# Scores from 40 rows a head and products on halves of 64 output rows, with a new list of first steps, in an mLSTM and feed-forward kernel

## The chip, the cores and the metric

The kernel runs on one core of a Trainium2 chip. The metric is device time of one execution in microseconds (us). The kernel before takes 456.23 us as the median of three runs (455.87 to 456.26). Lower is better.

## The reference

Two layers. The first is an mLSTM with 4 batches, 8 heads, 768 steps and a head size of 40; the second a feed-forward layer over its 3072 rows of 320 features, with 2048 hidden ones. Cut to what is computed:

```python
for t in range(S):                                   # S = 768
    m_new = np.maximum(f_gate[:, :, t] + m, i_gate[:, :, t])
    f_stab = np.exp(f_gate[:, :, t] + m - m_new)
    i_stab = np.exp(i_gate[:, :, t] - m_new)
    C = f_stab * C + i_stab * einsum('bhd,bhe->bhde', vt, kt)    # state, 40 x 40 a head
    n = f_stab * n + i_stab * kt
    h_tilde = einsum('bhde,bhe->bhd', C, qt)
    denom = np.maximum(np.abs(einsum('bhd,bhd->bh', n, qt)), 1.0)
    y[:, :, t] = sigmoid(o_gate[:, :, t]) * h_tilde / denom
x = y.transpose(0, 2, 1, 3).reshape(3072, 320)
h = x @ w_in                                         # 320 x 2048
out = (np.maximum(h, 0) + alpha * np.minimum(h, 0)) @ w_out      # 2048 x 320
```

All results are float32; the weights w_in and w_out come as float64.

## The kernel before

The steps over time are cut into chunks of 128 tokens: 6 chunks a batch, 24 in all. Inside a chunk the recurrence becomes products of matrices: scores (K times Q, 128 x 128 for each of 8 heads), weighed by a matrix of decays E, times the values; and a state part, Q times the state C that the chunks before left. Two chunks make a group of 256 tokens, for which the feed-forward layer is computed: products with the upper weights (`ph`, 8 pairs of hidden blocks, fp32r in parts), relu, and products with the lower weights (`po`).

The first six chunks (the first batch) are computed in f32 directly; the later ones from bf16 parts. The change touches the first six only. For them:

- Q and K of a chunk are transposed by pairs of heads on TensorE (steps qT and kT, tile `pqk`) and copied out by ScalarE (qc, kc). A pair's two heads stand in rows 0 to 39 and 64 to 103. Q goes to the tile `qf` whole. K goes to a padded tile `kf` with a place for each head of the pair: `padded_copy` writes the first head's 64 rows and the second head's 40 rows with two copies, and `padded_tiles` (step kfz) filled the other rows with zeros once.
- `scores(n, par)` (steps sc) multiplies K of one head of each pair, padded to 104 rows, with Q: four matmuls for each of the two heads of the pairs, in two separate steps. VectorE weighs them with E (wg).
- `values` (steps v) multiplies E, 128 rows by 128 columns, with the values `va` of 42 columns, for eight heads into one tile `pH`.
- `from_state` (steps fm, ft) multiplies `qf` with the state C of a pair, 84 columns, into `pI`.
- `products` (steps um, uc; tile `pu`) updates the state. It writes the two heads of a pair to rows 0 to 39 and 64 to 103 of its output. The change doesn't touch it.

The order of all instructions of each engine is written out by hand: `ORDER` lists steps by name, `PATTERN` goes on for the later groups, and `pin` ties each engine to that order. So an instruction that waits holds back everything behind it on its engine. Names in the list: dq, dv, dL, do are loads of q and k, of values, of the decay rows `Lb` and of the output gate; iXY, rX and oX with d, s, x, y, j, h, l or others behind them load a block of w_in or w_out (d), and take it apart from float64 (passes on ScalarE and VectorE, tiles `t_wi`, `t_wr`, `t_wo`) into high and low parts (h, l). U, R, S, G, K are the five steps of a feed-forward block of a group, D its lower products; warm2 are two matmuls on constants into a tile that nothing reads. i01 is the load into tile `wi_1` of the first rows, o4 and o3 are two blocks of w_out.

All loads stand on one queue, SP's, in the order of the list.

Of the kernel before, what the change touches and what calls it, by code (L numbers as in the profile page):

```python
# [8 lines left out]
F32 = mybir.dt.float32  # L9
# [8 lines left out]
def kernel(ctx: ExitStack, tc: tile.TileContext, q, k, v, i_gate, f_gate, o_gate, w_in, w_out, alpha, out):  # L18
    nc = tc.nc
    B, H, S, D = q.shape  # L20
    DM, DFF = w_in.shape
    P = 128
# [316 lines left out]
    def values(n, E, busy=lambda: None):  # L339

        pH = psa(f"pH{n}")
        dense(pH, FILL.get(n, 0))
        va = va_t[n // GC % NV][:, n % GC]
        for i in range(H):
            if i % 2 == 0:
                busy()
            par, p = divmod(i, NPR)
            h = 2 * p + par
            nc.tensor.matmul(  # L349
                pH[:, h * VA : (h + 1) * VA], E[par][:, p * P : (p + 1) * P], va[:, h], start=True, stop=True  # L350
            )
        return pH[:, : H * VA].rearrange("p (h e) -> p h e", e=VA)
# [48 lines left out]
    def from_state(n, qf, Q=None):  # L401
# [237 lines left out]
    def row_of(g, fp, e):  # L639
# [12 lines left out]
    FILL = {}  # L652
    ORDER = """warm14 dq0 Cz warm2 warm2 warm2 qT0 warm2 sca0 lf0a kT0 i00d lf0z lf0b li0 L0 sca1 bj0 dq1 warm2 qc0 lqa lqb kc0 lqc lqd sp01 eeL i00s
        lf1a lqe wt0 warm2 warm2 warm2 qT1 qc1 bTt bTc ex01 warm2 sp00 warm2 warm2 sp11 r0d lf1b ewj wTt wTc ex00 warm2
        sp10 ex11 kT1 i00y L1 li1 do0 dv0 kfz i01d eTt ex10 wd0 dq2 gma i00j sc00 o0d lpa sc01 um0 kc1 gmd gmm sc11
        eTc eel bj1 og1 r0s uc0 fm1 wtl wg01 sc10 ewl lpb i11d wd1 alT wg00 gmc qT2 i01s glt ft1 wg10 glc alC dL lpc
        lpd lpe qc2 warm2 wg11 dv1 um1 uc1 i00h i01x i01j kT2 kc2 i00p o0s o0x sp20 v0 r0y r0j gr0 sp21 fm2 dq3 ex20
        warm2 o0j r0h i01h ft2 i01p ex21 o0h warm2 gg0 r0l gx0 i11s sc20 wg20 v1 ta1 gr1 qT3 qc3 i11x gp0 x0 xa0 sc21
        dL4 gg1 gx1 gp1 kT3 wg21 x1 xa1 o1d wd3 xd0 r0H xd1 wd2 sq30 ey30 r0L i11j ex40 o0l F0 U00 i20d i10d R00 S00
        kc3 v2 ta2 um2 uc2 o1s o1y U01 dq4 i10s i10x i10j sq31 gr2 o1j i11k i11l ey31 qT4 G00 ex41 fm3 ft3 sc30 K00  # L660
        wg30 i10h um3 uc3 D00 R01 kT4 i20s do1 S01 qc4 wd4 kc4 o1h i20x sc31 wg31 dv2 um4 uc4 i20j og2 o2d i20h gg2
        i10p fm4 o1l o5d sc41 wg41 G01 K01 i21d gx2 r2d sc40 i20p o2s o2x dq5 wg40 o5s o5x v3 ta3 o2j gr3 gg3 o2h o5j
        r2s dL5 o4d r2x o2l U02 o3d r2j gx3 gp3 R02 gp2 i21s v4 ft4 ta4 qT5 qc5 r2H ex50 r2h r2p U03 x2 R03 S02 G02 x3
        dq6 i21y i21j r2L i31d fm5 ft5 xa2 xd2 i21h i21p dv3 i30d kT5 kc5 K02 S03 o4s o4y D01 G03 wd6 K03 o3s o3y o3j
        D02 do2 dL7 ex51 o7d o4j o6d U04 R04 S04 o3h xa3 V05 r05 o3p o4h sc50 o4p sc51 G04 i31s i31x xd3 s05 wg51 um6
        uc6 K04 gr4 wg50 F1 U10 U11 R10 S10 og3 gg4 gx4 dL6 gp4 R11 S11 G10 o5h o5p v5 K10 D10 U12 ta5 G11 g05 K11 vp0
        i31j i30s i30x gr5 gg5 U13 i31h i30j R12 i30h D11 S12 i31l G12 gx5 gp5 K12 D12 R13 dq7 S13 o7s i30l U06 o7x
        do3 o7j N05 G13 K13 D13 tp0 o6s tp1 o6x R06 tp2 x4 x5 o6j o6h vp1 U07 o7h tp3 D03 D04 D05 R07 S06 G06 S07 o6l
        xa5 xd5 xa4 xd4 G07 K06 K07 D06 o7l D07 Z0"""
    PATTERN = """og.-1 V4<< tf.1 vb.1 xn.-1 xp.-1 V5<< tg.1 g2<< N2<< vc.1 r4<< vb.0 th.1 ti.1 s4<< g3<< r5<< s0.0 s1.0 ua.0 ub.0  # L670
# [270 lines left out]
    def first_group():  # L941
# [140 lines left out]

        def scores(n, par):
            if n >= GC:
                ps = psa(f"pS{n}_{par}")
            elif n * par == 0:
                ps = ps_h.tile([P, 512], F32, tag="h", name=f"pS{n}_{par}")
            else:
                ps = ps_o.tile([P, 512], F32, tag="o1", name=f"pS{n}_{par}")
# [97 lines left out]
        def decay_parts(k, tag):  # L1187
# [35 lines left out]
        def values_of(n):  # L1223
            got["h", n] = values(n, [E[n, 0], E[n, 1]])
# [5 lines left out]
        def chunk_steps(n):  # L1230

            steps[f"wd{n}"] = lambda: weighed(n)
            steps[f"v{n}"] = lambda: values_of(n)
            steps[f"ta{n}"] = lambda: added(n)
# [8 lines left out]
            for par in range(2):  # L1243
# [121 lines left out]
```

## Time and profile before

| | |
|---|---|
| median of three runs | 456.23 us (455.87 to 456.26) |
| the profiled execution | 456.2 us |
| its span, first to last instruction | 454.5 us |
| TensorE busy | 448.2 us, 99% of the span |
| TensorE weight loads busy | 438.8 us, 97% |
| VectorE, ScalarE, GpSimd busy | 310.9, 314.9, 312.6 us (68%, 69%, 69%) |
| granted clock of TensorE, mean | 0.998 |
| moved by DMA | 61.60 MB, mean 136 GB/s |

Busy shares of the whole span are means over two very different stages. In the first some 85 us the first batch is computed while all weights are loaded and taken apart; then the pattern of the later groups repeats. A matmul of the trace lasts until its modelled end, which lies behind the next one's start, so a block's cost is read from its start to the start of the next block. An f32 matmul stands as two records in the trace, an fp32r or bf16 one as one.

### The profile page before, as it was taken

To read this page: it belongs to the slowest core of one execution; us is meant where nothing else is said; L and a number is where in the kernel's file an instruction comes from. 1 tells how busy PE (TensorE), PEld (TensorE's weight loads), DVE (VectorE), ACT (ScalarE), POOL (GpSimd) and SP (SyncE) were. 2 spreads that over 40 slices of the span, in tenths; PEclk is the share of its full clock that TensorE was granted. 3 is DMA by queue.
4 is the path that set the end of the run, shared out by engine and by line. 5 is a ranking of instruction groups with operands and counts; after the bars stand their busy time and mean duration, and the time that the engine had idled before them with its cause. 6 is when DMAs were issued, how large, how long until landed. Compare 5 with 4: busy or idle time off the path is not lost.

```text
span 454.5 us, 11766 instructions
## 1 busy us (share of the span) xinstructions
PE 448.2 (99%) x4418; PEld 438.8 (97%) x4418; DVE 310.9 (68%) x659; ACT 314.9 (69%) x717; POOL 312.6 (69%) x400
## 2 busy tenths in 40 slices
PE   8999999999999999999999999999999999999996
PEld 6789999999999999999999999999999999999996
DVE  4798999558866767767767767767767767753321
ACT  5999997959767767758768758658758668433331
POOL 7836566737889698588798698597798696143231
PEclk9999999999999999999999999999999999999999
DMA  8999998769674575597783783589682451000000
GB/s 182 248 253 214 232 232 226 139 143 180 156 168 110 137 160 104 133 184 163 121 183 103 131 179 105 115 188 180 128 168 86 97 142 40 1 30 1 30 1 29
DMA packets 156162, 61.60 MB, mean 136 GB/s; under 512 B 140154, under 2 KB 145834, under 8 KB 156106
## 3 DMA queue, kind: packets, MB, share of 16 engines
q1 hardware_dynamic: 156026, 60.75, 59.9%
q8 instruction: 35, 0.57, 0.5%
q14 instruction: 21, 0.17, 0.1%
q10 hardware_dynamic: 80, 0.11, 0.1%
HBM read 36.90 MB, written 4.03 MB: 90 GB/s over the span
## 4 chain that ended last, share of the span: by engine, by line
PE 91%; ACT 4%; DVE 3%; POOL 1%; issue 1%; POOLq 0%; DVEq 0%; ACTq 0%
PE po L771 36%; PE ph L734 5%; PE ph L739 5%; PE ph L735 5%; PE ph L736 5%; PE ph L741 5%; PE ph L737 5%; PE ph L740 5%; PE ph L738 5%; PE pH L390 4%; PE pS L491 4%; PE pu L192 2%; PE px L600 2%; PE pS L1092 2%; PE pH L349 2%; PE pI L415 1%
## 5 line engine op out<-in xcount | busy, mean ns | idle before, releaser
L760 POOL TENSOR_TENSOR gl<-g,gh 128x512 fp32r<-128x512 f32 x74 | 96.1, 1301 | 32.5 <-ACT gh L758 31.3
L744 ACT ACTIVATE g<-ph 128x512 f32<-128x512 f32 x96 | 57.3, 597 | 81.7 <-PE ph L741 79.7
L771 PE MATMUL po<-OH,gh 128*128 128x320 f32 x368 | 111.3, 314 | 0.0
L771 PE MATMUL po<-OL,gh 128*128 128x320 f32 x368 | 108.7, 308 | 0.0
L749 DVE SCALAR_TENSOR_TENSOR g<-g,oma,ph 128x256 f32<-128x256 f32 x148 | 63.6, 471 | 65.5 <-ACT g L744 64.1
L771 PEld LDWEIGHTS po<-OH,gh 128*128 128x128 f32 x368 | 69.2, 188 | 0.0
L771 PEld LDWEIGHTS po<-OL,gh 128*128 128x128 f32 x368 | 69.2, 188 | 0.0
L771 PE MATMUL po<-OH,gl 128*128 128x320 f32 x368 | 68.8, 308 | 0.0
L771 PEld LDWEIGHTS po<-OH,gl 128*128 128x128 f32 x368 | 57.5, 188 | 0.3 <-DVE gl L760 0.3
L734 PE MATMUL ph<-XH,WH 128*128 128x256 f32 x192 | 54.1, 282 | 0.5 <-DVE g L749 0.5
L735 PE MATMUL ph<-XH,WH 128*128 128x256 f32 x192 | 53.4, 278 | 0.0
L736 PE MATMUL ph<-XH,WL 128*128 128x256 f32 x192 | 53.2, 277 | 0.0
L739 PE MATMUL ph<-XL,WH 128*128 128x256 f32 x192 | 53.2, 277 | 0.0
L741 PE MATMUL ph<-XL,W 128*128 128x256 f32 x192 | 53.1, 277 | 0.0
L737 PE MATMUL ph<-XH,WL 128*128 128x256 f32 x192 | 53.1, 277 | 0.0
L738 PE MATMUL ph<-XH,W 128*128 128x256 f32 x192 | 53.1, 276 | 0.0
L740 PE MATMUL ph<-XL,WH 128*128 128x256 f32 x192 | 53.1, 276 | 0.0
L462 ACT ACTIVATE E<-Lb,gates 128x128 f32<-128x128 f32 x160 | 50.0, 393 | 0.0
L758 ACT CAST gh<-g 128x512 fp32r<-128x512 f32 x74 | 45.7, 618 | 4.0 <-PE po L771 2.4
L375 ACT CAST E<-pS 128x512 bf16<-128x512 f32 x72 | 41.1, 582 | 6.3 <-DVE pS L372 5.8
L465 POOL TENSOR_SCALAR_AFFINE_SELECT E<-E 128x512 f32<-128x512 f32 x40 | 27.0, 676 | 15.0 <-ACT E L462 14.4
L734 PEld LDWEIGHTS ph<-XH,WH 128*128 128x128 f32 x192 | 36.1, 188 | 0.6 <-ACT gh L758 0.6
(200 smaller groups left out, 1127.2 us busy)
## 6 DMA issues: line engine op xcount, KB each, us to landing
Lb<-L_d SPq DMA_DIRECT2D x20, 512.0 KB
wo<-in_moe_w_out_dram SPq DMA_DIRECT2D x8, 640.0 KB
wi<-in_moe_w_in_dram SPq DMA_DIRECT2D x8, 512.0 KB
qn<-in_q_dram SPq DMA_DIRECT2D x24, 160.0 KB
kn<-in_k_dram SPq DMA_DIRECT2D x24, 160.0 KB
og<-in_o_gate_dram SPq DMA_DIRECT2D x24, 160.0 KB
va<-in_v_dram SPq DMA_DIRECT2D x24, 160.0 KB
out_dram<-ob SPq DMA_DIRECT2D x11, 320.0 KB
```

The source lines that it names most:

```text
L734: nc.tensor.matmul(dst, WH[half][:, 0, hs], XH[:, 0], start=True, stop=False)
L735: nc.tensor.matmul(dst, WH[half][:, 1, hs], XH[:, 1], start=False, stop=False)
L736: nc.tensor.matmul(dst, WL[half][:, 0, hs], XH[:, 0], start=False, stop=False)
L737: nc.tensor.matmul(dst, WL[half][:, 1, hs], XH[:, 1], start=False, stop=False)
L738: nc.tensor.matmul(dst, W2[:, fs], XH[:, 2], start=False, stop=False)
L739: nc.tensor.matmul(dst, WH[half][:, 0, hs], XL[:, 0], start=False, stop=False)
L740: nc.tensor.matmul(dst, WH[half][:, 1, hs], XL[:, 1], start=False, stop=False)
L741: nc.tensor.matmul(dst, W2[:, fs], XL[:, 2], start=False, stop=True)
L744: nc.scalar.activation(gt, ph, AF.Relu, scale=-1.0)
L749: nc.vector.scalar_tensor_tensor(out=y[:, e], in0=gt[:, e], scalar=oma[:, f : f + 1], in1=ph[:, e], op0=ALU.mult, op1=ALU.add)
L760: (nc.vector if split else nc.gpsimd).tensor_tensor(gl, y, gh.bitcast(F32), ALU.subtract)
L771: nc.tensor.matmul(po[j], x[:, e, j * P : (j + 1) * P], W[f // NB][:, f % NB], **ends)
```

## The change

Scores take one step a chunk. K is copied once, to rows 0 to 103 of an unpadded tile, and each head's 40 rows are multiplied with the same 40 rows of Q, the two heads of a pair by turns into two tiles. The fills of the padding go. Values and state parts are computed in two halves of 64 output rows each, twice as many matmuls of half the columns of weights. And `ORDER` is laid out anew: 442 steps in place of 427, with 88 warm-up matmuls in place of 44, all of them ahead of the first feed-forward block.

```diff
+    halves = slice(0, P // 2), slice(P // 2, P)
...
-    kpads = []
-
-    def padded_tiles():
-
-
-        for K in kpads:
-            nc.gpsimd.memset(K[64:R, 0], 0.0)
-            nc.gpsimd.memset(K[:64, 1], 0.0)
...
-    def padded(n):
-        return kpads[(n + NDIR) % 2]
-
-    def padded_copy(K, pk):
-        nc.scalar.copy(K[:64, 0], pk[:64])
-        nc.scalar.copy(K[64:R, 1], pk[64:R])
...
     def values(n, E, busy=lambda: None):
...
-            nc.tensor.matmul(
-                pH[:, h * VA : (h + 1) * VA], E[par][:, p * P : (p + 1) * P], va[:, h], start=True, stop=True
-            )
+            for t in halves:
+                nc.tensor.matmul(
+                    pH[t, h * VA : (h + 1) * VA], E[par][:, p * P : (p + 1) * P][:, t], va[:, h], start=True, stop=True
+                )
...
     def from_state(n, qf, Q=None):
...
-                nc.tensor.matmul(pI[:, es], qf[:R, p * P : (p + 1) * P], C[:, es], start=True, stop=True)
+                for t in halves:
+                    nc.tensor.matmul(pI[t, es], qf[:R, p * P : (p + 1) * P][:, t], C[:, es], start=True, stop=True)
...
-    ORDER = """warm14 dq0 Cz warm2 warm2 warm2 qT0 warm2 sca0 lf0a kT0 i00d lf0z lf0b li0 L0 sca1 bj0 dq1 warm2 qc0 lqa lqb kc0 lqc lqd sp01 eeL i00s
+    ORDER = """warm14 dq0 Cz qT0 warm2 warm2 sca0 qc0 lf0z warm2 i00d kT0 lf0a r0d warm2 lf0b warm2 warm2 warm2 warm2 L0 i00s
...
-        for j in range(2):
-            kpads.append(sb.tile([P, 2, 512], F32, tag="kS", name=f"kf{j}", bufs=2))
+        keys = [sb.tile([P, 2, 512], F32, tag="kS", name=f"kf{j}", bufs=2)[:, 0] for j in range(2)]
...
             if j == 0:
-                qk[n] = sb.tile([P, 512], F32, tag="qf", name=f"qf{n}"), padded(n)
-                copy(qk[n][j][:R], pq[:R])
-            else:
-                padded_copy(qk[n][j], pq)
+                qk[n] = sb.tile([P, 512], F32, tag="qf", name=f"qf{n}"), keys[(n + NDIR) % 2]
+            copy(qk[n][j][:R], pq[:R])
...
-        def scores(n, par):
-            if n >= GC:
-                ps = psa(f"pS{n}_{par}")
...
+        def scores(n):
+
+            for par in range(2):
+                if n >= GC:
+                    ps = psa(f"pS{n}_{par}")
+                elif n * par == 0:
+                    ps = ps_h.tile([P, 512], F32, tag="h", name=f"pS{n}_{par}")
+                else:
+                    ps = ps_o.tile([P, 512], F32, tag="o1", name=f"pS{n}_{par}")
+                pS[n, par] = ps
             for p in range(NPR):
                 sl = slice(p * P, (p + 1) * P)
-                nc.tensor.matmul(ps[:, sl], qk[n][1][:R, par, sl], qk[n][0][:R, sl], start=True, stop=True)
-            pS[n, par] = ps
+                for par in range(2):
+                    r = slice(64 * par, 64 * par + D)
+                    nc.tensor.matmul(pS[n, par][:, sl], qk[n][1][r, sl], qk[n][0][r, sl], start=True, stop=True)
```

How the list moves instructions is seen in the program's order. TensorE, before, at the scores of chunk 0 (`pS` with tiles qf_188 and kf_131) and the first state update (`pu`):

```order
L273 MATMUL pqk_1_277<-ident,kn_80 104x128 x4
L996 MATMUL ps_ge_297<-ident,g_WH_95 128x32
L1092 MATMUL pS_0_310<-qf_188,kf_131 128x128 x4
L1092 MATMUL pS_1_319<-qf_188,kf_131 128x128 x4
L192 MATMUL pu_324<-va_81,kd_304 40x42 x8
L1182 MATMUL pg<-g_gd,unit 104x192
```

TensorE, now, at the same place (of the eight scores' rows the first two):

```order
L193 MATMUL pu_326<-va_81,kd_290 40x42 x8
L166 LDWEIGHTS const-bfloat16-1.0
L166 MATMUL warm<-const-bfloat16-1.0 128x256
L274 MATMUL pqk_1_339<-ident,kn_80 104x128 x4
L1083 MATMUL pS_0_344<-qf_165,kf_131 128x128
L1083 MATMUL pS_1_345<-qf_165,kf_131 128x128
L985 MATMUL ps_ge_354<-ident,g_WH_95 128x32
L1172 MATMUL pg<-g_gd,unit 104x192
```

The state update and the transposes of K (`pqk_1`, chunk 1) have moved ahead of chunk 0's scores; the update needs the first values, `va_81`.

SP's queue, before, its first loads (`wi_0` and `wi_1` are blocks of w_in, `wr` its last rows, `og` output gates):

```order
L111 DMA kn_79<-in_k_dram 128x8x40
L820 DMA wi_0_176<-in_moe_w_in_dram 128x1024
L111 DMA qn_78<-in_q_dram 128x8x40
L111 DMA kn_80<-in_k_dram 128x8x40
L820 DMA wr_250<-in_moe_w_in_dram 64x1024 x2
L140 DMA og_285<-in_o_gate_dram 128x8x40 x2
L124 DMA va_81<-in_v_dram 128x8x40 x2
L820 DMA wi_1_295<-in_moe_w_in_dram 128x1024
```

SP's queue, now:

```order
L112 DMA kn_79<-in_k_dram 128x8x40
L809 DMA wi_0_171<-in_moe_w_in_dram 128x1024
L809 DMA wr_180<-in_moe_w_in_dram 64x1024 x2
L112 DMA qn_78<-in_q_dram 128x8x40
L112 DMA kn_80<-in_k_dram 128x8x40
L809 DMA wi_1_226<-in_moe_w_in_dram 128x1024
L141 DMA og_297<-in_o_gate_dram 128x8x40 x2
L125 DMA va_81<-in_v_dram 128x8x40 x2
```

The block `wi_1` has moved ahead of the gates and of the values; `wr` ahead of chunk 1's q and k.

ScalarE, now, at two blocks of w_out. On SP's queue `wo_946` (o3) is issued first and `wo_979` (o4) next; before, the one issued first (`wo_841`) was used first:

```order
L851 CAST WH_851<-t_wi_1_920 128x512
L1012 COPY kf_132<-pqk_1_1046 104x512
L819 ACTIVATE t_wo_1057<-wo_979 128x640
L747 CAST gh_3_1076<-ph_3_991 128x512
L819 ACTIVATE t_wo_1083<-wo_946 128x640
```

The load that is issued second is used first, two instructions of ScalarE ahead of the other; K is copied in one instruction.

## Rows read from the trace of the kernel before

**Rows 1.** The page of the profiled execution: TensorE's busy time with its share and instructions and that of the other engines, and the chain of work that ended last, by engine.

```profile
PE 448.2 (99%) x4418; PEld 438.8 (97%) x4418; DVE 310.9 (68%) x659; ACT 314.9 (69%) x717; POOL 312.6 (69%) x400
...
PE 91%; ACT 4%; DVE 3%; POOL 1%; issue 1%; POOLq 0%; DVEq 0%; ACTq 0%
```

**Rows 2.** Timeline of TensorE, merged blocks of like instructions: start in us, duration in us to the end of the last one, line, operation, output and inputs, shape, count. What a block takes is counted from its start to the next one's.

```profile
14.22 2.05 PE L1092 MATMUL pS<-qf,kf 104*128 104x128 f32 x16
16.20 0.51 PE L192 MATMUL pu<-va,kd 128*40 128x42 f32 x16
16.64 0.57 PE L1182 MATMUL pg<-g_gd,unit 32*104 32x192 f32 x2
...
18.13 1.02 PE L409 MATMUL pI<-C,qf 104*128 104x84 f32 x8
18.98 1.09 PE L1092 MATMUL pS<-qf,kf 104*128 104x128 f32 x8
...
46.53 1.99 PE L1092 MATMUL pS<-qf,kf 104*128 104x128 f32 x16
48.35 1.88 PE L349 MATMUL pH<-va,E 128*128 128x42 f32 x16
50.06 0.36 PE L734 MATMUL ph<-XH,WH 128*128 128x256 f32 x1
```

**Rows 3.** The same timeline, at warm-up matmuls, at transposes by channel and at the longest wait up to 72 us; in brackets the idle time ahead and who ended it.

```profile
8.13 0.84 PE L165 MATMUL warm<-const-bfloat16-1.0 128*128 128x256 bf16 x6
8.81 0.60 PE L273 MATMUL pqk<-ident,qn 128*104 128x128 f32 x4
...
68.43 0.36 PE L734 MATMUL ph<-XH,WH 128*128 128x256 f32 x1 [0.47 <-DVE g L749]
```

**Rows 4.** Busy time by stretch: the stretch and its length, then busy us (and instructions) of TensorE, its weight load, VectorE, ScalarE and GpSimd, the granted share of TensorE's clock, the mean busy share of the DMA engines and GB/s moved.

```profile
36.00:45.00 9.00, 9.00 (x101) 8.68 (x100) 7.77 (x19) 8.32 (x20) 5.72 (x8) 1.00 0.97 227
45.00:60.00 15.00, 15.00 (x142) 14.83 (x142) 14.30 (x27) 14.05 (x27) 8.61 (x9) 1.00 0.94 226
60.00:72.00 12.00, 11.51 (x106) 11.02 (x105) 11.38 (x24) 10.43 (x23) 7.70 (x8) 1.00 1.02 252
72.00:85.00 13.00, 13.00 (x106) 13.00 (x105) 11.54 (x22) 11.37 (x21) 8.73 (x11) 1.00 0.76 174
85.00:100.00 15.00, 15.00 (x114) 14.99 (x113) 7.92 (x15) 10.55 (x29) 9.90 (x14) 1.00 0.59 128
```

**Rows 5.** Timeline of the DMA issues on SP's queue: start and duration of an issue.

```profile
45.29 5.01 SPq L131 DMA_DIRECT2D Lb<-L_d  x1
```

**Rows 6.** Instructions by tile and by line: durations in ns (least, median, most), first and last start, shape. Weight loads of the state update pu and of the scores pS.

```profile
L192 PEld LDWEIGHTS pu<-va,kd x96: 112/117/121, 16.2 to 67.7; 128*40 128x40 f32 x96
L1092 PEld LDWEIGHTS pS<-qf,kf x96: 186/192/192, 14.2 to 67.1; 104*128 104x128 f32 x96
```

**Rows 7.** Timeline of ScalarE: a copy of K by channel in two pieces.

```profile
15.29 0.57 ACT L329 COPY kf<-pqk 64x512 f32<-64x512 f32 x1
15.88 0.58 ACT L330 COPY kf<-pqk 40x512 f32<-40x512 f32 x1
```

**Rows 8.** Busy time by stretch as in rows 4, here for the last two columns, in three stretches of 15 us (that of 45 to 60 us stands in rows 4).

```profile
0.00:15.00 15.00, 13.08 (x90) 9.93 (x91) 7.85 (x17) 9.90 (x28) 12.31 (x32) 1.00 0.95 183
15.00:30.00 15.00, 15.00 (x155) 13.57 (x154) 12.61 (x30) 14.30 (x31) 8.80 (x11) 1.00 0.95 249
30.00:45.00 15.00, 14.71 (x148) 13.76 (x147) 13.30 (x30) 13.72 (x36) 8.93 (x12) 1.00 0.95 241
```

**Rows 9.** DMA issues by tile: output and input, queue, count, size of one (kn, va and og are as qn).

```profile
Lb<-L_d SPq DMA_DIRECT2D x20, 512.0 KB
wo<-in_moe_w_out_dram SPq DMA_DIRECT2D x8, 640.0 KB
wi<-in_moe_w_in_dram SPq DMA_DIRECT2D x8, 512.0 KB
qn<-in_q_dram SPq DMA_DIRECT2D x24, 160.0 KB
...
wr<-in_moe_w_in_dram SPq DMA_DIRECT2D x4, 256.0 KB
```

**Rows 10.** Timeline of VectorE: a pass over t_wi, the first weighing of scores, the first feed-forward's step, the second group's.

```profile
14.97 0.67 DVE L854 SCALAR_TENSOR_TENSOR t_wi<-wi,t_wi 128x512 uint32<-128x512 uint32 x1
...
17.46 1.29 DVE L1096 TENSOR_TENSOR E<-pS,E 128x512 f32<-128x512 f32 x2
...
35.98 1.00 DVE L749 SCALAR_TENSOR_TENSOR ph<-g,oma,ph 128x256 f32<-128x256 f32 x2
...
71.91 1.01 DVE L749 SCALAR_TENSOR_TENSOR ph<-g,oma,ph 128x256 f32<-128x256 f32 x2 [0.21 <-ACT g L744]
```

**Rows 11.** Waits of VectorE: who waited for whom, us in total, times, the longest. From 14 to 36 us the first and the last of the five that lie behind 17.46 us (the others: 0.4, 0.4 and 0.2), then from 36 to 72 us the first and the last of the four (the others: 0.6 and 0.2).

```profile
DVE E L1096 <- PE pS L1092: 0.4, 1, 0.4
...
DVE T L420 <- PE pI L409: 0.2, 1, 0.2
...
DVE t_wi L852 <- ACT wi L840: 0.7, 2, 0.4
...
DVE ph L749 <- ACT g L744: 0.2, 1, 0.2
```

**Rows 12.** Timeline of ScalarE: the first pass over o4's weights.

```profile
61.39 0.80 ACT L830 ACTIVATE t_wo<-wo 128x640 f32<-128x640 f32 x1
```

More of the change, by code (lines that the diff above doesn't have):

```diff
@@ L652 @@
     FILL = {}
-    ORDER = """warm14 dq0 Cz warm2 warm2 warm2 qT0 warm2 sca0 lf0a kT0 i00d lf0z lf0b li0 L0 sca1 bj0 dq1 warm2 qc0 lqa lqb kc0 lqc lqd sp01 eeL i00s
[L654 to L669, printed above, removed]
@@ new lines @@
+    ORDER = """warm14 dq0 Cz qT0 warm2 warm2 sca0 qc0 lf0z warm2 i00d kT0 lf0a r0d warm2 lf0b warm2 warm2 warm2 warm2 L0 i00s
+        warm2 lqa li0 warm2 eeL sca1 lqb lqc i00y lqd lf1a bj0 warm2 warm2 lqe dq1 sp01 i01d qT1 warm2 wt0 kc0
+        lf1b bTt bTc warm2 qc1 warm2 sp11 warm2 sp10 warm2 ewj warm2 warm2 wTt warm2 ex01 sp00 warm2 warm2 wTc
+        wd0 ex11 do0 warm2 ex00 li1 L1 warm2 warm2 gma dv0 ex10 warm2 gmd og1 um0 lpa warm2 kT1 sc0 eTt bj1 uc0
+        eTc gmm wg01 kc1 dq2 wd1 o0d alT eel fm1 wtl r0s alC sc1 ewl lpb i00j qT2 i00h ft1 lpc dv1 dL glt gmc
+        i01s lpd warm2 wg10 wg00 i01x um1 wg11 glc qc2 kT2 uc1 lpe kc2 warm2 i01j r0y i00p i11d r0j warm2 sp20
+        v0 o0s o0x warm2 sp21 o0j fm2 dL4 ex20 i01h r0h gr0 i01p gg0 ft2 i11x gx0 dq3 gp0 warm2 r0l ex21 o1d
+        i11s v1 wd2 warm2 warm2 qT3 qc3 sc2 ta1 x0 i10d xa0 gr1 gg1 warm2 o0h gx1 gp1 wg20 x1 i11j kT3 xa1 kc3
+        r0H xd1 xd0 wg21 F0 ex40 o0l warm2 r0L i11k warm2 U00 sq30 R00 S00 v2 ey30 sq31 dq4 o1s um2 U01 ta2 gr2
+        i10s o1y i10x uc2 G00 wd3 o1j ey31 i11l i10j fm3 qT4 wd4 ex41 um3 K00 o2d ft3 R01 kT4 qc4 S01 uc3 D00
+        i10h dv2 sc3 i20d kc4 i20s um4 do1 wg30 i20x wg31 i10p o1h o1l o2x o5d og2 i20j gg2 uc4 i20h G01 sc4 gx2
+        v3 ta3 o5s o2s o5x K01 wg40 gr3 fm4 o2j i20p wg41 i21d o2h r2d o5j dq5 o2l i21s gp2 ft4 gg3 U02 dL5 r2x
+        o3d qT5 r2s v4 gx3 r2j gp3 qc5 R02 o4d r2H ta4 ex50 dq6 U03 x2 S02 r2L r2h fm5 R03 G02 x3 i21y i31d i21j
+        r2p S03 xa2 K02 kT5 i21h kc5 ft5 dv3 o4s i21p dL7 D01 xd2 G03 o4y K03 do2 o3s wd6 o3y i30d D02 xa3 o3j
+        o4j U04 ex51 V05 o6d R04 o7d o3h xd3 r05 S04 o4h o3p G04 i31x o4p i31s sc5 um6 s05 uc6 K04 wg51 gr4 wg50
+        F1 U10 U11 R10 v5 S10 og3 gg4 dL6 R11 S11 G10 gx4 o5h o5p K10 D10 G11 g05 vp0 i30x ta5 U12 i31j K11 gr5
+        U13 i31h i30s D11 gg5 R12 S12 gx5 i30j o7x gp4 i31l G12 K12 i30h R13 gp5 D12 o7s i30l x4 U06 S13 G13 vp1
+        tp0 o6s dq7 o7j tp1 N05 K13 D13 o6x o6j U07 x5 tp2 R07 xa4 R06 xa5 D03 D04 o6h tp3 S06 D05 o7h xd4 do3
+        S07 G06 o6l K06 xd5 o7l G07 D06 K07 D07 Z0"""
@@ L1081, in first_group @@
         pS = {}
-        def scores(n, par):
-            if n >= GC:
-                ps = psa(f"pS{n}_{par}")
[L1086 to L1089, printed above, removed]
+        def scores(n):
[7 more added lines that the diff above has]
+                pS[n, par] = ps
             for p in range(NPR):
                 sl = slice(p * P, (p + 1) * P)
-                nc.tensor.matmul(ps[:, sl], qk[n][1][:R, par, sl], qk[n][0][:R, sl], start=True, stop=True)
-            pS[n, par] = ps
+                for par in range(2):
+                    r = slice(64 * par, 64 * par + D)
+                    nc.tensor.matmul(pS[n, par][:, sl], qk[n][1][r, sl], qk[n][0][r, sl], start=True, stop=True)
         def weigh(n, par):
@@ L1216, in first_group @@
             eeL=lambda: nc.scalar.activation(eL[:, P:GT], L[:, P:GT], AF.Exp),
-            kfz=padded_tiles, Cz=zero_states,
+            Cz=zero_states,
             og1=lambda: open_gate(0, 0, GC), og2=lambda: open_gate(0, GC, 2 * GC), og3=lambda: open_gate(0, 2 * GC, NC),
@@ L1232, in chunk_steps @@
             steps[f"wd{n}"] = lambda: weighed(n)
+            steps[f"sc{n}"] = lambda: scores(n)
             steps[f"v{n}"] = lambda: values_of(n)
@@ L1248, in chunk_steps @@
                 add(f"ex{n}{par}", lazily(lambda par=par: decay(n, par)))
-                steps[f"sc{n}{par}"] = lambda par=par: scores(n, par)
                 steps[f"wg{n}{par}"] = lambda par=par: weigh(n, par)
```

## The prediction

> **What bounds the kernel now.** I read the page first, then busy time by stretch, then the timelines, the waits and the DMA rates. The page gives 454.5 us from first to last instruction inside an execution of 456.2 us, so 1.7 us lie around the span; the median of the runs shown is 456.23, and I count against 456.2. TensorE is busy for 99% and makes 91% of the chain that ended last [rows 1]. A busy TensorE can be a waiting one, so the timelines decide: from 14.22 us on its blocks follow each other at their streaming rate [rows 2], and the longest wait up to 72 us is 0.47 us at 68.43 [rows 3]. But three other resources stand close behind. VectorE works 14.30 of 15 us between 45 and 60 us and 11.38 of 12 between 60 and 72 [rows 4]; ScalarE 14.05 and 10.43. The DMA engines are busy for 0.94 to 1.02 of every stretch up to 72 us [rows 4, 8], and one issue of a 512 KB load (Lb [rows 9]) holds its queue for 5.01 us at 45.29 [rows 5]. After 85 us only TensorE is full [rows 4]. So a saving on TensorE before 72 us counts only as far as VectorE and the loads can follow.
>
> **The change on TensorE.** Per chunk three blocks change. In [rows 2] each f32 matmul is two records. *Scores*: 16 records take 1.82 us where a values block follows (46.53 to 48.35), 0.11 us a record. Now the two heads of a pair stand in different halves of the rows and write different banks, so two records can run side by side. *Values*: 16 records in 1.71 us (48.35 to 50.06), 0.107 each; now 32 records on 64 columns, in pairs on different output halves. *State part*: 8 records, 0.85 us (18.13 to 18.98); now 16.
>
> The nearest row for such pairs is the state update pu, whose two heads already write different output halves: 16 records of 40 columns in 0.44 us (16.20 to 16.64), 0.055 per pair, and its weight load lasts 117 ns where a full one lasts 192 [rows 6]. Values: 16 pairs cost at least half of 0.107 each, 0.86 us, and at most pu's pair by 64/40 columns, 0.088, so 1.41; without any overlap they stay at 1.71. I take 0.95, a saving of 0.76: pu's own pair already holds the end of its block. Scores: 8 pairs at 0.11 are 0.90, without overlap 1.82; no row shows two row halves at work together; I take 1.0, by the likeness to pu, a saving of 0.8. State part: between 0.43 (half) and 0.85; I take 0.65, a saving of 0.2. In all 6 x 0.8 + 6 x 0.76 + 5 x 0.2 = 10.4 us.
>
> Against that stand the changes between tilings. A block of 16 scores ahead of pu takes 1.98 us (14.22 to 16.20), ahead of a full-width block 1.82 (46.53 to 48.35): up to 0.16 us per change [rows 2]. The change has 17 such blocks with two ends, some of them neighbours; I take 0.1, 34 x 0.1 = 3.4, between nothing and 5.4. The Trainium skill speaks against the change here: TensorEngine Tiling, section Key Properties, says that changing the tiling mode, and not only the tile, drains TensorE. The trace agrees, with those 0.16 us; with a drain of that size at each of the 34 ends the saving would shrink by another 2.0 us. For row halves the skill (TensorE: Matmul & The Clock Gate, Part 3) gives 3.07 times for four row tiles; no row here shows it.
>
> The new list has 34 warm-up matmuls after the last row spread ahead of chunk 0 (pb, sp00), the old one 6: 28 x 0.113 (six from 8.13 to 8.81 [rows 3]) = 3.1 us. All stand ahead of the first feed-forward block. Net 10.4 - 3.4 - 3.1 = 3.9 us on TensorE: after the first feed-forward block and up to the second group's (three chunks of each block, 5.3 less 18 x 0.1) 3.5 us; ahead of it (three blocks of scores, two of values, two state parts) 4.3 - 1.4 - 3.1, about nothing; 0.4 for the last values.
>
> **The change on the other engines.** ScalarE copies K by channel once instead of in two pieces; the second starts 0.59 us behind the first [rows 7], so 0.59 goes, six times, 3.5 us. GpSimd loses four fills of kf; it is busy for 5.72 of 9 us at 36 to 45 [rows 4], so I give them nothing. VectorE keeps its instructions. Nothing hides VectorE: it gains only what it waits.
>
> **Start to first feed-forward.** Here the new list costs. The first pu now stands ahead of chunk 0's scores, and pu needs chunk 0's values, whose load now stands behind the weight load wi_1. By bytes [rows 8, 9]: up to and with va the loads make 2.56 MB before and, with wi_1's 512 KB, 3.09 MB now; 183 GB/s x 15 us = 2.75 MB have moved at 15 us, then 249 GB/s, so va lands at about 14 us before and 16.4 now. Behind the waiting pu are queued, on TensorE, two warm-ups, the K transposes of chunk 1 and the scores; VectorE waits for pu and then for the scores. Pu 0.44, warm-ups 0.23 and transposes 0.5 (0.60 to the end of the like block at 8.81 [rows 3]) put the scores at 17.5, not 14.22, and with 1.0 for them and 0.17 for ps_ge, which VectorE takes first, the first weighing at 18.7, not 17.46 [rows 10]. One pass over t_wi, 0.6 us, which ran before it at 14.97 [rows 10], lies behind it now. Before, 18.5 us led from there to the first feed-forward's VectorE step at 35.98. If no wait goes: 18.7 + 18.5 + 0.6 = 37.8; if the five VectorE waits on TensorE that lie on the way go (0.4, 0.4, 0.4, 0.2 and 0.2, 1.6 in all [rows 11]): 36.2. Since TensorE has lost half of each of these blocks I take 1.2 of the 1.6: +0.6 us, bounds +0.2 and +1.8.
>
> **First feed-forward to the second group's (35.98 to 71.91).** TensorE offers 3.5 us. VectorE is idle 36 - (7.77 + 14.30 + 11.38) = 2.55 us there; its four listed waits are 0.7, 0.6, 0.2 and 0.2 [rows 11]. ScalarE gives three copies. I take the listed waits: -1.7, bounds 0 and -2.55. A load bounds it too: the new list uses o4's weights first, and these are the second of the pair, with 13.1 MB up to and with them (22 loads of 160 KB, 8 of 512, 4 of 256, 6 of 640 and 0.3 MB of small ones [rows 9]); 183, 249, 241 and 226 GB/s x 15 us = 13.5 MB had moved at 60 us [rows 4, 8], so they land no earlier than 60 - 0.4/0.226 = 58.3, against their use at 61.39 [rows 12]. That caps the gain there at 3.1 us; behind a wait there stand, on ScalarE, a gh and o3's pass, for which TensorE waits.
>
> **To the end.** Chunk 5's values save 0.4 to 0.76 on TensorE; VectorE has 13 - 11.54 = 1.46 us idle to 85 us, then room. I take -0.6, bounds 0 and -1.5. Sum: +0.6 - 1.7 - 0.6 = -1.7, so 454.5 us. The worst ends give 458.0, the best +0.2 - 2.55 - 1.46, 452.4.
>
> **Rivals.**
> *TensorE's saving comes through whole.* For it: TensorE is the chain's 91%, and waits on other engines hardly show. Then 456.2 - 3.9 = 452.3. Against: VectorE would have to be busy without a gap, beyond its best stretch of 14.30 in 15.
> *Row halves do not overlap.* Nothing in the trace shows that they do. Six blocks stay at 1.8 us and pay their ends: the first feed-forward comes at +1.8, the stage behind offers 3.5 - 2.4 = 1.1, the end 0.3: 456.2 + 1.8 - 1.1 - 0.3 = 456.6.
> *The late start is not recovered (slower).* Place: pu ahead of chunk 0's scores, behind va. Price +1.8 at the first feed-forward; if the later waits only change their owner (a load like o4's in place of TensorE), 456.2 + 1.8 - 0.6 = 457.4. It decides if the first feed-forward's VectorE step is later than 37.5 us. For it: loads back to back up to 72 us. Against: VectorE's waits on TensorE are real and go.
>
> **How the numbers follow.** Forecast 0.50, whole saving 0.17, row halves 0.13, late start 0.20. A measurement of this kernel tells about 0.2% (0.9 us) from no change. Faster than 455.3: the whole saving and nine tenths of the forecast, 0.62; the row halves, the rest of the forecast and some late starts are within, 0.21; slower 0.17. The forecast's own range is 453.3 to 455.5; with the rivals 452.0 to 457.4.
>
> **What would show it.** In the changed profile: a scores block of 16 records in 0.9 to 1.1 us with starts in pairs, a values block in 0.9 to 1.1, a state part in 0.6 to 0.8; single K copies; the first pu at 16 to 17 us and the first feed-forward's VectorE step at 36.2 to 37.8; TensorE with waits for VectorE or ScalarE between 36 and 72 us that it has not now; VectorE at or above 95% there; ScalarE near o4's load at 58 to 60 us. I am wrong if scores still take 1.8 us, if VectorE's step of the second group comes before 69.3 or after 72 us, or if the granted clock falls under full speed in the first stage, where 14 warm-ups stand ahead of the first transposes, not 20.

## The result and the profile after

The changed kernel takes 459.45 us as the median of six runs (458.24 to 460.02), the kernel before 456.16 over its six (455.87 to 456.26): 1.0070 times, interval 1.0056 to 1.0083, so 3.3 us slower. Forecast were 454.5 us, and 452.0 to 457.4 with all rivals; the result lies outside both. The profiled execution took 458.87 us, its span is 457.1: 2.6 us more than the span of 454.5 before; its granted clock is 1.00, that of the other runs 0.996 to 1.00.

The page, as in [rows 1]: TensorE is as busy as before, but holds less of the chain.

```profile
PE 448.0 (98%) x4598; PEld 434.6 (95%) x4598; DVE 308.8 (68%) x659; ACT 310.9 (68%) x711; POOL 308.0 (67%) x396
...
PE 86%; ACT 3%; DVE 3%; SPq 3%; DMA 2%; POOL 1%; issue 1%; POOLq 0%; DVEq 0%
```

Timeline of TensorE in the first 27 us, as in [rows 2].

```profile
17.27 0.51 PE L193 MATMUL pu<-va,kd 128*40 128x42 f32 x16 [1.03 <-DMA va<-in_v_dram]
...
18.47 1.16 PE L1083 MATMUL pS<-qf,kf 40*128 40x128 f32 x16
19.56 0.24 PE L985 MATMUL ps_ge<-ident,g_WH 32*128 32x32 f32 x1
...
20.14 0.80 PE L396 MATMUL pI<-C,qf 104*64 104x84 f32 x16
20.88 1.16 PE L1083 MATMUL pS<-qf,kf 40*128 40x128 f32 x16
...
25.04 1.13 PE L335 MATMUL pH<-va,E 128*64 128x42 f32 x32
26.11 0.39 PE L166 MATMUL warm<-const-bfloat16-1.0 128*128 128x256 bf16 x2
```

From start to the next start, 16 scores take 1.09 us (18.47 to 19.56) where they took 1.82, values 1.07 (25.04 to 26.11) for 1.71, a state part 0.74 (20.14 to 20.88) for 0.85. Inside the block of scores at 18.47 the sixteen starts come in pairs 7 ns apart, and from the second pair on a pair every 0.11 us; before, single records stood 0.11 us apart. So the blocks are as fast as forecast, row halves do overlap, and the first pu waits for the values' load as forecast.

VectorE's steps of [rows 10]: the first weighing, the first feed-forward's step, the second group's.

```profile
19.95 0.68 DVE L1086 TENSOR_TENSOR E<-pS,E 128x512 f32<-128x512 f32 x1
...
37.71 1.01 DVE L738 SCALAR_TENSOR_TENSOR ph<-g,oma,ph 128x256 f32<-128x256 f32 x2
...
71.19 1.01 DVE L738 SCALAR_TENSOR_TENSOR ph<-g,oma,ph 128x256 f32<-128x256 f32 x2 [0.20 <-ACT g L733]
```

The first step is 1.73 us late (35.98 before), the second 0.72 early (71.91 before). Up to there the change gains. Busy time by stretch, as in [rows 4]:

```profile
36.00:45.00 9.00, 8.86 (x132) 8.03 (x131) 8.71 (x17) 9.00 (x25) 6.59 (x9) 1.00 0.92 217
45.00:60.00 15.00, 14.22 (x204) 12.90 (x203) 14.45 (x30) 13.35 (x26) 7.42 (x10) 1.00 0.92 260
60.00:72.00 12.00, 11.78 (x125) 11.20 (x125) 11.58 (x26) 10.98 (x25) 8.93 (x8) 1.00 0.91 235
```

TensorE is no longer full (14.22 of 15 us); VectorE nearly is (14.45), and ScalarE is in the first row (9.00 of 9). What is lost lies behind. Take the start of each block of lower products, `po`, and count from the start of the same block before: -1.1 us at 73 us, -0.4 at 106, +0.6 at 125, and then an ever growing distance, +1.1 at 194, +2.1 at 334, +2.7 at 426, though TensorE, VectorE, ScalarE and GpSimd run the same instructions in the same order from 98 us on.

Two places show most of the why; the 0.7 us between 73 and 106 us are not traced to a cause. TensorE at 113.69 us, and the issues on SP's queue ahead of it (after, then before):

```profile
113.69 1.05 PE L478 MATMUL pS<-qS,kS 120*128 120x128 bf16 x16 [0.77 <-DMA kS<-kS]
```

```profile
97.35 4.52 SPq L141 DMA_DIRECT2D og<-in_o_gate_dram  x6
...
111.20 0.75 SPq L310 DMA_DIRECT2D kS<-kS  x1
```

```profile
79.39 5.26 SPq L140 DMA_DIRECT2D og<-in_o_gate_dram  x6
...
106.31 0.74 SPq L309 DMA_DIRECT2D kS<-kS  x1
```

The six loads of the next batch's gates (step do3) went out at 79.39 before, ahead of the transposes of chunks 6 and 7. Now they stand behind those, hold the queue from 97.35 on, and the last copy that fills kS is issued at 111.20, not 106.31; TensorE waits 0.77 us for it.

The other place is the pace of the upper products `ph`. The first two rows of a block of 32 and the row behind it, after, then before:

```profile
147.62 0.28 PE L723 MATMUL ph<-XH,WH 128*128 128x256 f32 x1
147.74 0.28 PE L724 MATMUL ph<-XH,WH 128*128 128x256 f32 x1
...
151.39 0.31 PE L760 MATMUL po<-OH,gh 128*128 128x320 f32 x1
```

```profile
146.95 0.28 PE L734 MATMUL ph<-XH,WH 128*128 128x256 f32 x1
147.07 0.28 PE L735 MATMUL ph<-XH,WH 128*128 128x256 f32 x1
...
150.58 0.31 PE L771 MATMUL po<-OH,gh 128*128 128x320 f32 x1
```

32 matmuls take 3.77 us now, 117.8 ns each, and 3.63 before, 113.4. Same instructions, same order, no wait, clock 1.00. A later group has its eight pairs of hidden blocks in five blocks of ph. Two of them run at the slow pace in every such group, U0 with U1 (the one shown) and U3; U2, U4 with U5 and U6 with U7 keep the old one. `po` of D4, D6 and D7 takes 146.2 to 147.5 ns a matmul for 145.3 to 145.6.

### The profile page after: what moved, and what is told of

Its sections match the earlier page's. It is cut to its first block, busy times and chain, and to the rows that moved or that the text cites. A ratio compares the mean times of both kernels' runs of the same rounds, so it can differ in the third digit from the quotient of the medians.

```text
span 457.1 us, 12106 instructions
## 1 busy us (share of the span) xinstructions
PE 448.0 (98%) x4598; PEld 434.6 (95%) x4598; DVE 308.8 (68%) x659; ACT 310.9 (68%) x711; POOL 308.0 (67%) x396
## 4 chain that ended last, share of the span: by engine, by line
PE 86%; ACT 3%; DVE 3%; SPq 3%; DMA 2%; POOL 1%; issue 1%; POOLq 0%; DVEq 0%
PE po L760 35%; PE ph L723 5%; PE ph L724 5%; PE ph L730 5%; PE ph L726 5%; PE ph L725 5%; PE ph L728 5%; PE ph L727 5%; PE ph L729 5%; PE pH L376 4%; PE pS L478 3%; PE px L587 2%; DMA va<-in_v_dram 1%; PE pI L402 1%; PE pu L193 1%; SPq L809 1%
## 5 line engine op out<-in xcount | busy, mean ns | idle before, releaser
L760 PEld LDWEIGHTS po<-OL,gh 128*128 128x128 f32 x368 | 69.3, 188 | 0.3 <-DVE OL L855 0.3
L434 POOL TENSOR_TENSOR og<-og,r 128x320 f32<-128x320 f32 x18 | 13.0, 723 | 34.7 <-DVE r L427 32.9
```

What stands on the lines that cost most here:

```text
L760: nc.tensor.matmul(po[j], x[:, e, j * P : (j + 1) * P], W[f // NB][:, f % NB], **ends)
```

## The experiments

Three theories stood at the start. A: three separate losses, all of them the list's (a late start, the gate loads, the pace). B: the blocks themselves cost it. C: it is all the late start, which shows again at whatever waits last.

**blocks_alone.** The old list; only the blocks are exchanged:

```diff
-i00j sc00 o0d lpa sc01 um0
+i00j sc0 o0d lpa um0
...
-do0 dv0 kfz li1
+do0 dv0 li1
```

> The old list with the new blocks only: each chunk's two steps of scores become the one new step, at the place of the first of them (chunk 1: of the second), and the fills of the padding go; no load, no warm-up and no other step moves, and the tiles of the later groups stay where the kernel before has them, but for the banks of some of the mLSTM's products. Theory A (three losses, all of the list: a late start, the six gate loads behind the transposes, a slower pace of the upper products ph): none of them is here, TensorE keeps most of what it saves where VectorE can follow, 452.5 to 455 us. Theory B (the blocks themselves cost it, by their changes of tiling, or by slowing the products behind them): 457 us or more, with ph blocks at 118 ns a matmul after 120 us. Theory C (late start that is never won back): 454 to 456.

Measured: 461.68 us, 1.0120 times (1.0104 to 1.0135). No theory had this. A's time is missed by 6.7 us; B's time holds without its sign, since the ph blocks behind 120 us run at 113.4 ns. The distance to before is +6.16 us at 106 us and at 426; 6.0 of it stand at 74 us already. Busy time by stretch, then TensorE:

```profile
14.00:18.00 4.00, 1.71 (x33) 1.44 (x34) 4.00 (x6) 3.93 (x11) 3.08 (x3) 1.00 1.02 233
18.00:23.00 5.00, 4.98 (x38) 4.08 (x39) 3.30 (x7) 1.74 (x4) 2.51 (x4) 0.51 1.00 295
23.00:28.00 5.00, 5.00 (x52) 3.96 (x52) 3.60 (x8) 3.41 (x6) 1.28 (x1) 0.50 0.88 175
```

```profile
18.02 0.85 PE L1170 MATMUL pg<-g_gd,unit 32*104 32x192 f32 x2 [2.31 <-DVE gates L987]
...
20.11 2.08 PE L1081 MATMUL pS<-qf,kf 40*128 40x128 f32 x16
22.12 0.28 PE L1146 MATMUL pa<-ident,al 16*128 16x16 f32 x1
```

TensorE waits 2.31 us, then its clock is granted at half, 1.2 GHz in place of 2.4, until 28 us, and a block of scores takes 2.01 us (20.11 to 22.12), more than the old one. Why TensorE waits is seen on VectorE and GpSimd (VectorE here, GpSimd here, GpSimd before):

```profile
15.01 1.75 DVE L841 SCALAR_TENSOR_TENSOR t_wi<-wi,t_wi 128x512 uint32<-128x512 uint32 x1
16.68 1.19 DVE L1163 TENSOR_TENSOR g_gd<-ident,gam 32x192 f32<-32x192 f32 x1
```

```profile
14.84 1.37 POOL L1201 TENSOR_TENSOR g_WH<-g_li,g_L 32x512 f32<-32x512 f32 x1 [1.56 <-DVE g_L L1136]
16.28 1.38 POOL L975 TENSOR_TENSOR g_WL<-g_WH,g_L 32x512 f32<-32x512 f32 x1
```

```profile
14.62 0.52 POOL L318 MEMSET kf<- 40x512 f32 x1
15.18 0.52 POOL L319 MEMSET kf<- 64x512 f32 x1
15.67 1.39 POOL L1213 TENSOR_TENSOR g_WH<-g_li,g_L 32x512 f32<-32x512 f32 x1
```

The pass over t_wi takes 1.75 us; it took 0.67 at 14.97 [rows 10]. Then GpSimd filled the padding; now the fills are gone and its TENSOR_TENSOR comes 0.83 us earlier, beside that pass. The Trainium skill (SBUF — State Buffer, section SBUF: two separate sides) says that a VectorE instruction with two SBUF inputs and a GpSimd instruction that reads SBUF exclude each other; the trace agrees: 0.67 us beside fills, which only write, 1.75 beside one that reads. The next VectorE step, g_gd, took 0.34 us before, at 15.58, and takes 1.19 beside GpSimd's next TENSOR_TENSOR. The two are 1.9 us longer together, and the copy that TensorE waits for stands right behind them. That this makes the wait was not tried by itself. Nor is it the only wait: at 44 to 48 us TensorE waits for VectorE again, 2.1 us for a weighing, and the clock is at 0.60 from 48 to 52.

**gate_loads_back, ph_bank_back, values_first.** One step of the new list each: do3 behind dq7; the weighings wg10 and wg00 exchanged, which moves ph to its old bank of PSUM in every group; the load of wi_1 (i01d) behind that of the values (dv0).

```diff
-tp0 o6s dq7 o7j
+tp0 o6s dq7 do3 o7j
...
-wg10 wg00
+wg00 wg10
...
-i01d qT1
+qT1
-gma dv0 ex10
+gma dv0 i01d ex10
```

> The changed kernel with one step of its list moved back: the six loads of the next batch's output gates (do3) stand on SP's queue ahead of the transposes of chunks 6 and 7 again, as in the kernel before. Theory A: the 0.8 us for which TensorE waits at 113.7 us for kS goes, 458.3 to 458.8 us against the changed kernel's 459.45; the pace of ph after 120 us stays at 118 ns in two of five blocks of a group. Theory C (the loss is the late start, which shows at whatever waits last): another wait takes the place of that one, 459.2 or more.

Measured: 458.50 us, 1.0042 (1.0028 to 1.0056), against 1.0070 (1.0056 to 1.0083) for the changed kernel: the intervals only touch. The wait for kS is gone and nothing takes its place; the pace stays at 118. As theory A has it, against C.

> The changed kernel with the two weighings of scores wg10 and wg00 in the other order on VectorE, which gives the upper products ph of every group the bank of PSUM that they have in the kernel before, and changes no other place in memory. Theory A1 (the bank sets the pace): all ph blocks after 120 us run at 113 to 114.5 ns a matmul, 457.0 to 457.6 us. Theory A2 (the pace is set by where tiles lie in SBUF, or by what stands ahead of a block): two of five blocks of a group stay at 118, 459.0 to 459.7. Theory C: no change of the pace matters, 459.4.

Measured: 459.67 us, 1.0076 (1.0061 to 1.0091), the same two of five blocks at the slow pace, the first at 117.8 ns. The bank is not it.

> The changed kernel with the load of wi_1 (i01d) put back behind the first values' load (dv0), so that the values land about 2 us earlier. Theory A: the first pu no longer waits (1.03 us at 17.27), the first ph block starts at 33.5 to 34.2 us in place of 34.83; what reaches the end is at most that, 458.5 to 459.4 us. Theory C (the late start is the loss): as much as the start gains also reaches the end, 458 or less, and the wait for kS at 113.7 goes with it.

Measured: 459.17 us, 1.0066 (1.0050 to 1.0083), not told apart from the changed kernel. The first pu does not wait for the values; it comes at 17.29 all the same, since TensorE stood 1.21 us ahead of chunk 1's transposes in this execution. The first ph starts at 34.48 (34.83), later than the 34.2 that theory A allowed, and what the start gains is taken by the wait for kS, 1.2 us for 0.8. Theory C, by which that wait would go, falls.

**places_back, places_swapped.** What differs behind 125 us is where tiles lie. The kernel lays gaps between the tiles of w_out by hand:

```python
    GAP = dict(OL0=16, OH1=16, OH2=32, OL1=48, OH3=48, OL3=16, OL2=32)
```

A tile gets its place when it is first used. The old list uses OL3's room first (i20 is staged there), OL2's (i10) behind it; the new list the other way. Each takes 5120 bytes of a partition, with a gap of 64 bytes ahead of OL3 and of 128 ahead of OL2 (16 and 32 numbers of f32). So OL2 now lies where OL3 was, 64 bytes further on, and OL3 where OL2 was. places_back lays OL3 first in the changed kernel, places_swapped OL2 first in the kernel before:

```diff
     def staging(name, tag):
+        if tag == "OL2" and "OL3" in GAP:
+            gap("OL3")
+            const.tile([P, NB * DM], U32, tag="OL3", name="first_OL3")
         gap(tag)
```

> The changed kernel, where OL2 and OL3 (low parts of w_out, moving operands of a quarter of the lower products each) lie at the same bytes of SBUF as in the kernel before; every instruction and its order stay. Theory P (the new list uses the staging room of OL2 ahead of that of OL3, so the gaps that are laid between the tiles no longer fit, and po and the ph blocks behind it fall into a slower pace): after 120 us all ph blocks run at 113 to 115 ns a matmul, the distance to the kernel before stays level from 125 us to the end in place of growing by 2.2 us, 457.0 to 457.6 us. Theory Q (the pace comes from elsewhere: other tiles, or the phase in which the engines meet): U0, U1 and U3 stay at 118, 459.2 to 459.7.

> The kernel before, with OL2 and OL3 where the changed kernel has them, and nothing else changed. Theory P: its ph blocks U0, U1 and U3 of the later groups go to 118 ns a matmul, and it loses about 2 us from 120 us to the end, 458.0 to 458.6 us against 456.24. Theory Q: 456.0 to 456.5.

Measured: 457.72 us, 1.0036 (1.0023 to 1.0049), and 458.55, 1.0055 (1.0040 to 1.0070). The same block of ph, places_back, then places_swapped:

```profile
148.26 0.28 PE L726 MATMUL ph<-XH,WH 128*128 128x256 f32 x1
...
151.90 0.31 PE L763 MATMUL po<-OH,gh 128*128 128x320 f32 x1
```

```profile
147.07 0.28 PE L737 MATMUL ph<-XH,WH 128*128 128x256 f32 x1
...
150.84 0.31 PE L774 MATMUL po<-OH,gh 128*128 128x320 f32 x1
```

3.64 us and 3.77: the slow pace follows the two tiles into the old kernel and leaves the new one. In places_back the distance to before is level, +1.31 us at 125 and +1.37 at 426; in places_swapped it grows from +0.1 to +2.2. Theory P holds both ways; its 457.0 to 457.6 for places_back is missed by 0.1 us. ph does not even read these tiles: four of the twelve matmuls of each D4 to D7 do. U0 stands right behind D5 and U3 behind D7, but U2, behind D6, keeps the old pace, so how the pace gets from po to ph is not shown. Why these bytes are slow stays open too.

**blocks_alone_warm.** blocks_alone with 20 warm-ups in the wait.

```diff
-sc0 o0d lpa um0 kc1
+sc0 o0d lpa um0 warm20 kc1
```

> The old list with the new blocks (blocks_alone, 461.68 us) and 20 more warm-ups behind the first state update, where TensorE there waits 2.31 us for VectorE; they take 2.3 us at full clock, inside that wait. Theory W (what cost 6.2 us there is the clock that fell to half from 18 to 28 us behind that wait): the granted clock stays at 1.00 in every stretch, the first ph starts at 32.3 to 34 us in place of 36.77, 455.5 to 458.5 us. Rival (the blocks are slow in themselves, the clock only shows it): the first ph stays later than 35.5 us, 460 or more.

Measured: 458.56 us, 1.0051 (1.0036 to 1.0066), 3.1 us less. Theory W holds for the start: the first ph starts at 33.75, and the clock stays at 1.00 up to 29 us. It does not hold for the whole: the clock falls to 0.61 from 29 to 32, and TensorE still waits for VectorE later, 2.0 us at a pu and 1.6 us at transposes (2.1 and 1.6 in blocks_alone). So warm-ups in that wait gave back 3.1 of 5.4 us, and the old list has more such places than one.

**three_back, q1_ahead_too, fewer_warmups, warmups_at_q3.** All of them the changed kernel with OL2 and OL3 in place, do3 behind dq7, i01d behind dv0; then, one by one, r0d behind dq1; ten of the twelve warm-ups ahead of um0 left out; these ten put ahead of chunk 3's transposes.

```diff
-lf0a r0d warm2 lf0b
+lf0a warm2 lf0b
-bj0 warm2 warm2 lqe dq1
+bj0 warm2 warm2 lqe dq1 r0d
...
-sp00 warm2 warm2 wTc wd0 ex11 do0 warm2 ex00 li1 L1 warm2 warm2 gma dv0 i01d ex10 warm2 gmd og1 um0
+sp00 warm2 wTc wd0 ex11 do0 ex00 li1 L1 gma dv0 i01d ex10 gmd og1 um0
...
-warm2 warm2 qT3
+warm2 warm2 warm10 qT3
```

> The changed kernel with three of its losses undone at once: OL2 and OL3 in their old places, the six gate loads ahead of the transposes of chunks 6 and 7, and wi_1's load behind the first values. If they are separate, their gains add up: 2.2 + 1.0 + 0.3 = 3.5 us, 455.5 to 456.5 us, which is the kernel before within its measurement: then new blocks and new list win what the start loses and no more. If one hides behind another, 457 or more.

Measured: 455.85 us, 0.9998 (0.9986 to 1.0010). They add up, as far as the runs tell (454.85 to 457.94 us here): 3.6 us gained, 1.7 + 1.0 + 0.3 = 3.0 by the three alone, so none hides behind another. Its profiled execution (454.85 us, its fastest) keeps -1.3 us against before from 106 us to the end.

> three_back, and the load wr (r0d, 512 KB) behind the loads of chunk 1's q and k (dq1), as in the kernel before. In the profiles so far TensorE waits for chunk 1's q at 11 us, for 1.0 us in three_back, 1.7 in places_back, 2.3 in gate_loads_back, and in the last two the granted clock falls behind that wait. Theory L (the late q1 is a part of the late start, and its chance landing is what spreads the runs over 3 us): that wait is under 0.4 us, the clock stays at 1.00 in each run, the runs lie within 1 us of each other, and the median comes down from 455.85 to 454.3 to 455.0 us, under the kernel before. Rival (values or gates are what the start waits for anyway): 455.5 or more, spread as before.

Measured: 454.93 us, 0.9986 (0.9971 to 1.0002), not told apart from three_back by the intervals. TensorE's wait for chunk 1's q at 11 us, shown here in places_back and in three_back, is gone:

```profile
11.31 0.85 PE L277 MATMUL pqk<-ident,qn 128*104 128x128 f32 x4 [1.71 <-DMA qn<-in_q_dram]
...
10.87 0.62 PE L277 MATMUL pqk<-ident,qn 128*104 128x128 f32 x4 [1.03 <-DMA qn<-in_q_dram]
```

The median is as theory L expected, the spread is not: ten of twelve runs lie within 1.5 us, two are at 457.7 and 458.1 with a granted clock of 0.993.

> q1_ahead_too with ten of the twelve warm-ups left out that stand right ahead of the first state update (1.13 us at 0.113 each). If they are on the path, as the prediction had it, the first pu comes 1.1 us earlier, VectorE's first weighing about 0.6 earlier (it is then bound by its own steps and by the values' landing), and the end 0.3 to 0.6 us earlier, 453.9 to 454.6. If they only fill a wait that is there anyway (for the values, or for VectorE), 0.0 +- 0.3. If they hold the clock: it falls between 12 and 24 us and the median rises by 1 us or more.

Measured: 454.48 us, 0.9977 (0.9963 to 0.9990), not told apart from q1_ahead_too. The median lies in the range for warm-ups on the path, but the interval allows no change as well. The first pu comes 0.87 us earlier, but chunk 3's transposes at the same time (q1_ahead_too, then fewer_warmups):

```profile
15.62 0.51 PE L196 MATMUL pu<-va,kd 128*40 128x42 f32 x16
30.05 0.62 PE L277 MATMUL pqk<-ident,qn 128*104 128x128 f32 x4 [1.35 <-DVE r L426]
```

```profile
14.75 0.51 PE L196 MATMUL pu<-va,kd 128*40 128x42 f32 x16
30.02 0.62 PE L277 MATMUL pqk<-ident,qn 128*104 128x128 f32 x4 [1.33 <-DVE r L426]
```

The profile puts this wait down to VectorE, but the load of chunk 3's q ends it: its last piece lands at 29.91 and 29.89 us, and TensorE starts 0.14 us later, as it does in three_back behind chunk 1's q (10.73 to 10.87). So a load takes the gain. In this execution of fewer_warmups the clock falls behind that wait; in that of q1_ahead_too, behind one as long, it stays at 1.00:

```profile
28.00:30.00 2.00, 0.69 (x10) 0.34 (x7) 1.88 (x4) 1.60 (x6) 1.95 (x3) 1.00 0.74 167
30.00:32.00 2.00, 1.98 (x23) 1.70 (x24) 1.43 (x4) 0.58 (x1) 0.24 (x1) 1.00 1.02 330
32.00:34.00 2.00, 2.00 (x11) 1.57 (x10) 1.36 (x3) 1.69 (x5) 0.00 (x0) 0.52 0.98 236
```

> fewer_warmups with the ten warm-ups put back elsewhere: into the wait of 1.33 us for which TensorE stands ahead of chunk 3's transposes (28.7 to 30.0 us); in the profile of fewer_warmups the granted clock falls to 0.52 right behind it (32 to 34 us), in that of q1_ahead_too it does not. Theory G (what is left of the spread, single runs at 457 to 458 us, is the clock that falls behind this wait): the clock is 1.00 in each run, no run is over 455.5 us, the median is 454.2 to 454.6. Rival (other waits drop it too): the spread stays, median 454.5. If the ten are on the path: 455 or more.

Measured: 454.85 us, 0.9977 (0.9966 to 0.9987). The clock is 0.999 or 1.00 in all eight runs and none is over 456.2; but two are over 455.5, so the clock is not all of the spread, and the median is above the 454.2 to 454.6 of theory G. fewer_warmups and warmups_at_q3 are the two that beat the kernel before, each by 0.23%.

**values_full_width.** q1_ahead_too, with values and state parts in full width as before the change.

```diff
-            for t in halves:
-                nc.tensor.matmul(pH[t, h * VA : (h + 1) * VA], E[par][:, p * P : (p + 1) * P][:, t], va[:, h], start=True, stop=True)
+            nc.tensor.matmul(pH[:, h * VA : (h + 1) * VA], E[par][:, p * P : (p + 1) * P], va[:, h], start=True, stop=True)
```

> q1_ahead_too with the values and the state parts in full width again (16 records each of 128 columns, 8 for a state part); only the scores are new. On TensorE that is 0.64 us more for each of six values blocks and 0.1 for each of five state parts, 4.3 us. If TensorE's saving reaches the end: 458.5 or more. If VectorE bounds the first stage (my step for 36 to 72 us): a third of it or less, up to 456.0; without any effect, as in q1_ahead_too.

Measured: 457.32 us, 1.0039 (1.0019 to 1.0059), 2.4 us over q1_ahead_too. Of 4.3 us on TensorE about half reaches the end: more than the third that I expected if VectorE bounds the stage, less than all. The clock is a small part of it: by the runs at 0.999 or 1.00 alone the two medians are 456.8 and 454.7.

## Why the prediction was wrong

- **The blocks' prices were right.** Scores 1.09 us (taken 1.0 and 0.1 for each of two ends), values 1.07 (0.95), state part 0.74 (0.65). The drain of 0.16 at every end, which the Trainium skill's sentence (TensorEngine Tiling, section Key Properties) was weighed with, would make scores 0.90 + 0.32 = 1.22; the rows show 0.19 for both ends together.
- **Start to first feed-forward: mis-sized, inside its bounds.** +0.6 forecast, +1.73 measured (37.71 against 35.98), bounds +0.2 to +1.8. The first pu, which waits for the values, came at 17.27, not 16.4, and the first weighing at 19.95, not 18.7. That meets the late start's condition (later than 37.5), but what followed was not its course.
- **First feed-forward to the second group's: right in kind, near its bound.** -1.7 forecast, -0.72 - 1.73 = -2.45 measured, bound -2.55; VectorE has waits of 0.3 and 0.2 us left there, for 1.7 [rows 11], and o4's pass comes at 61.31 (61.39 [rows 12]).
- **"To the end. I take -0.6" is the step that failed.** From 71 us to the end it is +3.3 in the profiled execution (2.6 over the span, and the 0.7 gained by then), against bounds of 0 and -1.5. I counted only the last values and VectorE's room there, and put the rest of the program at nothing because its instructions stay. Two things that the list decides were not looked at: that do3 moved behind the transposes on SP's queue (0.95 us by gate_loads_back), though I followed that queue to o3 and o4; and that the order of first uses decides where tiles lie (1.7 us by places_back, 2.4 in the old kernel). The rest, some 0.6 us, is not traced. No rival held either.
- **The warm-ups were counted as a cost alone, 3.1 us.** blocks_alone, with the old list and its fewer warm-ups, shows another side: there the saved TensorE time turns into waits, the clock falls behind two of them, and the kernel is 5.4 us slower than before; 20 warm-ups in the first wait give 3.1 us back. In the new list, leaving out ten gave nothing that could be measured.
- **"GpSimd loses four fills, I give them nothing"** may be wrong where the list stays: in the kernel before the fills stand beside a VectorE pass that is 1.1 us longer beside a reading GpSimd step in blocks_alone. It was not tried by itself.
- The rival of the late start came nearest in time (457.4) and has the wrong cause: the start is won back by 72 us, and what is lost later could be undone without touching it.
- With those losses undone and two loads of the start moved back the kernel takes 454.5 to 454.9 us (q1_ahead_too, fewer_warmups, warmups_at_q3), about the 454.5 forecast. That is another list than the one forecast, so it does not save the sum.
- None of the three signs that I had named for being wrong turned up (scores at 1.8 us, VectorE's step outside 69.3 to 72, a lower clock in the first stage of the profile). All of them looked at the first 72 us.

## What to carry to other kernels

When a list or planner changes the order of first uses, compare the places of tiles in SBUF as well as the instructions: a pace that differs in blocks with the same instructions and no wait is the sign of it, and it costs in every later pass, here 0.24 us in each of nine groups. Time that TensorE gives back in a stage that other engines bound can become a wait, and the wait may cost the clock, as in blocks_alone; there it paid to fill it. Follow every load of the new list on its queue until the last one that moved, not only those of the stage that is speeded up.

## What the runs showed of the hardware

Two tiles of 5 KB a partition, exchanged and one of them 64 bytes further on, change the pace of matmuls that don't read them from 113.4 to 117.8 ns, in whole blocks, the same ones in every group from 125 us on; matmuls of the blocks that do read them go from 145.3 to 145.6 ns to 146.2 to 147.5. Two heads in different row halves give 1.82 / 1.09 = 1.67 times the rate, both ends of the block included. And a wait of TensorE can cost more than its length: behind one of 2.31 us in blocks_alone the clock was granted at half for some 10 us, and scores took 2.01 us for 1.09. Behind one of 1.33 us it fell in one execution, and behind one of 1.35 us in another it did not.
